# Seven products in place of eight for the second FFN product of chunks 2 to 6

## The chip, the cores and the metric

The kernel runs on one core of a Trainium2 chip. The metric is the time of one execution on the device, in microseconds (us). Each engine (PE for matmuls, DVE, ACT and POOL for work on elements, SP for DMA issues) takes its instructions from a queue of its own, and they wait for each other by semaphores.

## The reference

Eight batches of eight heads with 576 tokens each go through windowed attention; the heads' outputs side by side are the 4608 x 512 input `x` of a gated FFN.

```python
mask_plain = (rel >= 0) & (rel < 32)                        # heads 0 to 3
mask_dil = (rel >= 0) & (rel < 128) & (rel % 4 == 0)        # heads 4 to 7
attn = softmax(where(mask, q @ k.T / 8, -1e9));  x = heads of (attn @ v), joined
out = (gelu(x @ w_gate) * (x @ w_val)) @ w_out              # 512 -> 1536 -> 512
```

## The kernel before, in words

The FFN goes through nine chunks of 512 tokens, 0 to 8. A chunk has two stages on PE.

The **G stage** (L616 to L623) computes twelve blocks `nb` of 128 hidden columns. A block takes four matmuls of 512 columns for the gate and four for the value (`kc` 0 to 3, one for each quarter of `x` transposed, `xT`), each half in a PSUM bank that `gate_banks` (L816) names, which even and odd blocks use in turn. ACT then computes gelu of the gate (`g`, L872), and DVE multiplies it with the value into `u_all` (`u`, L877).

The **out stage** multiplies `u_all` with `w_out`. In chunks 1 to 6 it does so directly: four token tiles of twelve matmuls of 512 columns in banks 0 and 7 in turn, each tile copied out by ACT or DVE (`store`, L638; words w0, w1, w2, e3) and sent by SP. Chunks 7 and 8 (`SEVEN`, L822) cut both matrices into 2 x 2 blocks and compute seven block products of twelve matmuls of 256 columns, instead of eight (L674 to L706). For that DVE forms sums of neighbouring u blocks (`k`, L662) and once, in chunk 6, sums of the weights (`K`, L647); the partial results go through `snap` (three SBUF tiles), `part_out` (words q0 to q6) and `part_sum` (words s0 to s2).

The attention of batch c+1 lies in the out stage of chunk c (c = 1 to 6), as four pairs of heads i, j, k, l. S computes scores (PE), P takes their exp (ACT), M masks (DVE), D the denominators (PE), l and r their log and the exp of its negative (ACT), N the numerators (PE), and X divides into `xT` (DVE). So chunk c+1's G stage can't finish its first blocks before the last X of chunk c; `firsts` (L970) gives the order of its first sixteen matmuls. In batch 3 (chunk 2) pairs k and l are plain heads, from batch 4 on dilated ones.

The order of all work is written out by hand as words (`gate_words` L910, `out_words` L935), which `run_program` emits one by one. A number means so many of the stage's matmuls; any other word puts its instructions at the end of their engines' queues. Nothing reorders them afterwards. A chunk's loads (`F`, `H`, in chunk 2 `R`) stand at the head of its G words: SP issues the loads of q, k (staged in f32), the DMA transposes of their f16 copies, and the loads of v, for the batch after next; its queue then takes the chunk's output stores. POOL casts the staged q, k to f16, and v (`cast_part`, L302). Batch 4's v is cast at the end of `load_rest` (L298 to L300); for batches 5 to 7 the words v0 (dilated half) and v1 (plain half) in the out stages of chunks 3 to 5 do it.

The output rows of chunk 8 end with `last_products` (L742), which computes the seventh product in three parts, so that the last store is small.

Of the kernel before, what the change touches and what calls it, by code (L numbers as in the profile page):

```python
# [10 lines left out]
F32 = mybir.dt.float32  # L11
# [10 lines left out]
def kernel(  # L22
# [679 lines left out]

    def seven(banks):

        order = ((1, 3, True), (0, 4, True), (1, 5, False), (0, 1, False), (1, 2, True), (0, 7, False), (1, 6, True))
        return [mm for b, kind, first in order for mm in products(banks[b], kind, first)]  # L706

    def part_out(c, what, eng, banks):

        src, by = ps[:, banks[0 if what in (1, 3, 5) else 1], :], 1.0 / USCALE  # L710
        m3, a, f = snap
        dst = {0: m3, 1: a, 3: f}.get(what)
        osb = None
        if dst is None:
            osb = osbp.tile([P, DM], F32, tag="osb")
            dst = osb
        if what < 4:
            if eng:
                nc.scalar.activation(dst, src, AF.Copy, bias=0.0, scale=by)  # L719
            else:  # L720
                nc.vector.tensor_scalar(dst, src, by, None, ALU.mult)
        else:
            other, op = {4: (a, ALU.add), 5: (m3, ALU.subtract), 6: (f, ALU.add)}[what]
            nc.vector.scalar_tensor_tensor(dst, src, by, other, ALU.mult, op)  # L724
# [6 lines left out]
    def part_sum(what, eng):  # L731

        m3, a, f = snap
        e = nc.vector if eng else nc.gpsimd
        if what == 0:
            e.tensor_tensor(f, f, m3, ALU.add)  # L736
        elif what == 1:
            e.tensor_tensor(m3, tiles["O", 2], m3, ALU.subtract)
        else:
            e.tensor_tensor(f, f, tiles["O", 4], ALU.subtract)  # L740

    def last_products(c):  # L742

        for p, c0, c1, bank in ((0, 0, HM, 3), (1, 0, P, 5), (1, P, HM, 6)):
            for j, (s, t) in enumerate(operands(6)):
                src = ps[:, bank, 0 : c1 - c0]
                nc.tensor.matmul(src, s[:, P * p : P * p + P], t[:, c0:c1], start=j == 0, stop=j == NKP - 1)
            osb = osbp.tile([P, DM], F32, tag="osb")
            dst, rest = osb[:, 0 : c1 - c0], snap[2][:, HM * p + c0 : HM * p + c1]
            nc.vector.scalar_tensor_tensor(dst, src, 1.0 / USCALE, rest, ALU.mult, ALU.add)  # L750
            t0 = c * CH + 256 + P * p
            (nc.scalar if c0 else nc.sync).dma_start(out=out[t0 : t0 + P, HM + c0 : HM + c1], in_=dst)
# [100 lines left out]
    def run_program(c, words, mms, banks):  # L853

        units = {"S": two_s, "M": two_m, "D": two_den, "N": two_num, "T": two_t, "B": two_b, "X": two_x, "A": two_a, "l": two_l, "r": two_r, "P": two_p_of, "t": turn_first, "y": turn_second, "c": cast_six, "W": idle, "b": bias_first}
        joint = {"S": two_s_mms, "D": two_den_mms, "N": two_num_mms}
        for word in words.split():
            kind, args = word[0], [] if "+" in word else [int(x) for x in word[1:].split("@") if x]
            if "+" in word:
                lists = []  # L860
                for part in word.split("+"):
                    n, at = (int(x) for x in part[1:].split("@"))
                    lists.append((joint[part[0]](n, at), odd(n)))
                emit_tiles(*lists)
            elif kind.isdigit():
                for _ in range(int(word)):
                    mms.pop(0)()
            elif kind in units:
                units[kind](*args)
            elif kind == "g":  # L870
                g = ffn.tile([P, CH], F16, tag="g")
                nc.scalar.activation(g, ps[:, gate_banks(c, args[0])[0], :], AF.Gelu)  # L872
                tiles["g", args[0]] = g
            elif kind == "u":
                nb = args[0]
                val = ps[:, gate_banks(c, nb)[1], :]
                nc.vector.scalar_tensor_tensor(u_all[:, nb, :], tiles.pop(("g", nb)), USCALE, val, ALU.mult, ALU.mult)  # L877
            elif kind in "ew":
                at = args[1] if len(args) > 1 else c
                store(at, args[0], out_banks(at)[args[0]], "act" if kind == "e" else "dve")  # L880
            elif kind == "k":
                u_sums(*args)
            elif kind == "K":
                weight_sums(*args)
            elif kind == "q":
                part_out(c, args[0], args[1], banks)
            elif kind == "s":
                part_sum(*args)
            elif kind == "L":
                mms.clear()  # L890
                last_products(c)
            elif kind == "V":
                (second, second_v)[args[0] if args else 0]()
            elif kind == "v":
                cast_part(c + 2, args[0], tiles["M"])
            elif kind == "F":
                load_first(args[0])
            elif kind == "H":
                load_rest(args[0])
            elif kind == "R":  # L900
                load_rest(3)
                load_first(4)
                load_rest(4)
            elif kind == "E":
                nc.scalar.preload_act_table_set("natural_log_exp_and_others")
            else:
                nc.scalar.preload_act_table_set("gelu_and_others")  # L907
        assert not mms

    def gate_words(c):  # L910
# [22 lines left out]
        return f"{before} {loads} 7 G 3 g0 1 u0 1 g1 4 u1{sums[1]} {rest} 4 g{NNB - 1} 4{last}"  # L933

    def out_words(c):  # L935

# [19 lines left out]
        first = f"1 u11 4 S{i}@1+S{j}@4 E P{i} P{j} M{i} M{j} 7 w0 5" if c < 3 else f"E P{i} P{j} 1 u11 M{i} M{j}{v0} 12 w0 3"
        after = f"S{l + 1}@12+S{l + 2}@15" if 1 < c < 6 else ""
# [50 lines left out]
```

## Time and profile before

| | |
|---|---|
| median of 3 runs | 325.67 us (325.59 to 326.34) |
| profiled execution | 325.92 us, span 324.2 us |
| PE busy | 317.5 us, 98% of the span |
| DVE, ACT, POOL busy | 173.6, 159.1, 87.7 us |
| a G stage | 20.72 us on PE |
| out stages of chunks 2, 3 to 5, 6, 7 | 14.07, 13.30 to 13.31, 12.91, 9.17 us |

The span runs from the first to the last instruction; the time has 1.7 us more around it. Stages are read off the chain of work that ended last, which lists PE's groups with their starts. A matmul's shown end includes its way through the array, so a short one behind long ones ends a little early and the next long one a little late; only sums over a stage are exact.

### The profile page before, as it was taken

How to read it: one execution, taken by the hardware profiler on the slowest of the kernel's cores; microseconds unless marked ns; L12 is line 12 of the kernel's file. 1: busy time of each engine (PE TensorE's matmuls, PEld its weight loads, DVE VectorE, ACT ScalarE, POOL GpSimd, SP SyncE). 2: the span in 40 equal slices, each digit the busy share in tenths (PEclk: the TensorE clock that was granted, in tenths of full speed). 3: DMA queues.
4: the chain of work that ended last, by engine and by line, in shares of the span. 5: the costliest groups of instructions: out<-in, count | busy, mean ns of one | idle time of the engine just before them, and what ended most of it. 6: DMA issues, size and time to landing. Idle time of an engine off the chain costs nothing.

```text
span 324.2 us, 7943 instructions
## 1 busy us (share of the span) xinstructions
PE 317.5 (98%) x3273; PEld 162.6 (50%) x3273; DVE 173.6 (54%) x287; ACT 159.1 (49%) x239; POOL 87.7 (27%) x138
## 2 busy tenths in 40 slices
PE   7999999999999999999999999999999999999995
PEld 4754544444544454445444454445444544684474
DVE  6764646435543355436543554446676467636654
ACT  2673567434653557347633764366535753333320
POOL 8785703402491422231124111411000000040001
PEclk9999999999999999999999999999999999999999
DMA  8999997998899898898389627973000210021003
GB/s 190 183 198 207 205 192 154 268 185 193 194 253 207 214 198 237 191 223 183 126 191 242 161 78 178 249 169 111 32 3 0 92 42 0 0 84 47 2 1 129
DMA packets 107700, 47.11 MB, mean 145 GB/s; under 512 B 83600, under 2 KB 104080, under 8 KB 107664
## 3 DMA queue, kind: packets, MB, share of 16 engines
q1 hardware_dynamic: 94160, 38.29, 51.1%
q0 software_dynamic: 12944, 7.67, 16.6%
q10 hardware_dynamic: 560, 0.66, 0.7%
q8 instruction: 25, 0.41, 0.5%
q14 instruction: 11, 0.09, 0.1%
HBM read 37.75 MB, written 9.44 MB: 146 GB/s over the span
## 4 chain that ended last, share of the span: by engine, by line
PE 92%; DMA 4%; DVE 1%; POOL 1%; issue 0%; DVEq 0%
PE ps L623 58%; PE ps L630 23%; PE ps L458 6%; PE ps L696 5%; DMA wg<-in_moe_w_gate_dram 2%; DMA xT<-in_q_dram 2%; POOL xT L182 0%; DVE turned L740 0%; PE ps L378 0%; DVE osb L724 0%; PE ps L398 0%; DVE osb L750 0%; POOL band L123 0%; DVE ones L67 0%; PE ps L447 0%
## 5 line engine op out<-in xcount | busy, mean ns | idle before, releaser
L877 DVE SCALAR_TENSOR_TENSOR u_all<-g,ps 128x512 f16<-128x512 f16 x108 | 74.2, 688 | 93.3 <-PE ps L623 76.2
L872 ACT ACTIVATE g<-ps 128x512 f16<-128x512 f32 x108 | 63.6, 597 | 105.3 <-PE ps L623 105.3
L623 PE MATMUL ps<-xT,wg 128*128 128x512 f16 x432 | 112.5, 379 | 0.2 <-DMA wg<-in_moe_w_gate_dram 0.2
L623 PE MATMUL ps<-xT,wv 128*128 128x512 f16 x432 | 112.3, 379 | 0.0
L630 PE MATMUL ps<-wo,u_all 128*128 128x512 f16 x336 | 77.8, 380 | 0.0
L623 PEld LDWEIGHTS <-wv 128*128 128x128 f16 x432 | 42.1, 98 | 51.0 <-DMA wv<-in_moe_w_val_dram 0.6
L623 PEld LDWEIGHTS <-wg 128*128 128x128 f16 x432 | 42.1, 98 | 50.5 <-DMA wg<-in_moe_w_gate_dram 0.3
L630 PEld LDWEIGHTS <-u_all 128*128 128x128 f16 x336 | 30.8, 98 | 35.6 <-issue 0.5
L614 DVE TENSOR_TENSOR xT<-ps,rb 128x576 f16<-128x576 f32 x32 | 28.7, 936 | 16.2 <-PE ps L458 12.9
L488 ACT ACTIVATE P<-ps 128x832 f16<-128x832 f32 (+1 forms) x32 | 25.3, 835 | 15.8 <-PE ps L458 15.7
L217 POOL CAST s<-stage 128x640 f16<-128x640 f32 x24 | 17.3, 747 | 53.5 <-DMA stage<-in_q_dram 38.9
L254 POOL CAST v<-stage 128x1152 f16<-128x1152 f32 x11 | 13.0, 1184 | 62.0 <-DMA stage<-in_v_dram 43.5
L585 ACT ACTIVATE lg<-ps 128x576 f32<-128x576 f32 x30 | 18.7, 653 | 11.4 <-DVE xT L614 8.8
L591 ACT ACTIVATE rb<-lg 128x576 f32<-128x576 f32 x30 | 19.5, 690 | 0.3
L736 POOL TENSOR_TENSOR turned<-turned,vdiag 128x512 f32<-128x512 f32 x1 | 1.3, 1262 | 65.6 <-ACT turned L719 65.6
L229 POOL CAST s<-stage 128x512 f16<-128x512 f32 x24 | 14.4, 629 | 8.6 <-DMA stage<-in_q_dram 6.7
L643 DVE TENSOR_SCALAR osb<-ps 128x512 f32<-128x512 f32 x21 | 14.4, 685 | 2.6 <-PE ps L630 2.0
L493 DVE TENSOR_TENSOR P<-P,two_p 128x832 f16<-128x832 f16 x14 | 8.6, 612 | 10.9 <-ACT P L488 10.9
L493 DVE TENSOR_TENSOR P<-P,two_d 128x768 f16<-128x768 f16 x14 | 9.1, 664 | 9.8 <-ACT P L488 9.2
L907 ACT ACT_TABLE_LOAD x9 | 11.5, 1283 | 0.2
L458 PEld LDWEIGHTS <-v 64*64 64x64 f16 x616 | 7.7, 107 | 6.2 <-issue 5.1
L458 PEld LDWEIGHTS <-q 64*64 64x64 f16 x576 | 7.9, 107 | 5.3 <-issue 3.7
(90 smaller groups left out, 208.0 us busy)
## 6 DMA issues: line engine op xcount, KB each, us to landing
out_dram<-osb SPq DMA_DIRECT2D x35, 256.0 KB, 2.2
stage<-in_v_dram SPq DMA_DIRECT2D x28, 144.0 KB, 3.6
stage<-in_q_dram SPq DMA_DIRECT2D x24, 128.0 KB, 3.6
stage<-in_k_dram SPq DMA_DIRECT2D x24, 128.0 KB, 2.9
stage<-in_q_dram SPq DMA_DIRECT2D x6, 512.0 KB, 5.1
stage<-in_k_dram SPq DMA_DIRECT2D x6, 512.0 KB, 5.3
stage<-in_v_dram SPq DMA_DIRECT2D x20, 128.0 KB, 2.9
wo<-in_moe_w_out_dram POOLq DMA_DIRECT2D x3, 512.0 KB, 16.2
```

The lines of the kernel that those rows point to most:

```text
L217: nc.gpsimd.tensor_copy(s16[:, 1280 * t + 640 * g : 1280 * t + 640 * g + 640].rearrange("p (k c) -> p k c", k=5), st_of(i).rearrange("p (k ...
L458: nc.tensor.matmul(o[cols], lhs[rows], rhs[rows], start=st, stop=end, skip_group_check=True)
L488: nc.scalar.activation(pt[:, 0 : src.shape[1]], src, AF.Exp, bias=0.0, scale=scale)
L493: tiles["M"] = nc.vector.tensor_tensor(pt, pt, mask, ALU.mult)
L585: nc.scalar.activation(lg, psf[:, c0 : c0 + S], AF.Ln)
L591: nc.scalar.activation(rb, tiles.pop(("lg", n)), AF.Exp, scale=-1.0)
L614: nc.vector.tensor_tensor(dst, num, rb, ALU.mult)
L623: nc.tensor.matmul(ps[:, bank, :], w[:, kc, ns], xT[kc][:, tok], start=first, stop=end)
L630: nc.tensor.matmul(ps[:, bank, :], u_all[:, fc, tb * P : (tb + 1) * P], wo_t[fc // 4][:, fc % 4, :], start=(fc == 0), stop=(fc == NNB - 1),)
L696: lambda s=s, t=t, p=p, st=first and j == 0 and p == 0, end=j == NKP - 1: nc.tensor.matmul(ps[:, bank, HM * p : HM * p + HM], s[:, P * p : ...
L872: nc.scalar.activation(g, ps[:, gate_banks(c, args[0])[0], :], AF.Gelu)
L877: nc.vector.scalar_tensor_tensor(u_all[:, nb, :], tiles.pop(("g", nb)), USCALE, val, ALU.mult, ALU.mult)
```

## The change

The seven-product scheme is used in chunks 2 to 8. What goes with it:

- The products come in another order, M4, M5, M1, M3, M7, M2, M6, in two banks in turn. M5 is copied out before M3 is added onto its bank, so a partial M5 is kept; likewise M4 before M1. In chunks 2 to 6 q1 and q3 are on ACT and the other copies on DVE; s0 to s2 are on POOL. In chunk 7 s0 to s2 are on DVE.
- `part_sum` always adds into the third tile of `snap`: M4 + M1, minus M5, plus the second quarter of the output, minus the third one. q6 adds M6 to it.
- The sums of the weights move from chunk 6 to chunk 1, and the out stages of chunks 2 to 6 are redrawn: all four S of a batch stand in its own out stage, and none for the next.
- Batch 4's v is no longer cast in `load_rest` but by v0 and v1 in chunk 2's out stage; v0 and v1 now stand behind s1 and ahead of s2 in the words.
- Odd blocks use banks 3 and 6 instead of 1 and 4, and the first sixteen matmuls of chunks 3 to 7 have new orders.
- Chunk 8 has an out stage of its own, `last_chunk`, over banks 1, 2, 4, 5 and at the end 0, 7, 2, with M7 last in three parts.

```diff
-        if b < 5:
+        if b < 4:
             for part in range(0 if by_pool else 2):
                 cast_part(b, part)
...
-        order = ((1, 3, True), (0, 4, True), (1, 5, False), (0, 1, False), (1, 2, True), (0, 7, False), (1, 6, True))
+        order = ((1, 4, True), (0, 5, True), (1, 1, False), (0, 3, False), (1, 7, False), (0, 2, True), (1, 6, True))
...
-        dst = {0: m3, 1: a, 3: f}.get(what)
...
+        kept = {0: 0, 1: 1, 2: 2}.get(what)
...
-            other, op = {4: (a, ALU.add), 5: (m3, ALU.subtract), 6: (f, ALU.add)}[what]
+            other, op = {4: (snap[1], ALU.subtract), 5: (snap[0], ALU.add), 6: (snap[2], ALU.add)}[what]
...
+    def part_sum(what, eng, behind=0):
+
+        other, op = ((snap[1], ALU.subtract), (tiles.get(("O", 3)), ALU.add), (tiles.get(("O", 5)), ALU.subtract))[what]
+        ins = (nc.vector if eng else nc.gpsimd).tensor_tensor(snap[2], snap[2], other, op)
+        if behind:
+            tc.add_manual_dep(ins.ins, tiles["M"].ins.name, SYNC, reason="masks first")
+
+    def last_chunk(c):
...
+        run(2, 4, True)
+        nc.scalar.activation(a, ps[:, 2, :], AF.Copy, bias=0.0, scale=by)
+        run(5, 5, True)
+        nc.scalar.activation(e, ps[:, 5, :], AF.Copy, bias=0.0, scale=by)
+        run(1, 2, True)
+        c21 = osbp.tile([P, DM], F32, tag="osb", name="c21")
+        nc.vector.scalar_tensor_tensor(c21, ps[:, 1, :], by, a, ALU.mult, ALU.add)
+        sends(c21, 5)
+        run(2, 1, False)
+        nc.scalar.activation(f, ps[:, 2, :], AF.Copy, bias=0.0, scale=by)
+        run(5, 3, False)
+        nc.vector.tensor_tensor(f, f, e, ALU.subtract)
+        nc.vector.tensor_tensor(a, f, c21, ALU.subtract)
+        c12 = osbp.tile([P, DM], F32, tag="osb", name="c12")
+        nc.scalar.activation(c12, ps[:, 5, :], AF.Copy, bias=0.0, scale=by)
+        sends(c12, 3)
+        nc.vector.tensor_tensor(a, a, c12, ALU.add)
+        run(4, 6, True)
+        c22 = osbp.tile([P, DM], F32, tag="osb", name="c22")
+        nc.vector.scalar_tensor_tensor(c22, ps[:, 4, :], by, a, ALU.mult, ALU.add)
+        sends(c22, 6)
+        for p, c0, c1, bank in ((0, 0, HM, 0), (1, 0, P, 7), (1, P, HM, 2)):
...
-        return ((0, 7), (1, 6) if c == 1 else (1, 4))[nb % 2]
+        return ((0, 7), (1, 6) if c == 1 else (3, 6))[nb % 2]
-    SEVEN = range(7, NCH)
+    SEVEN = range(2, NCH)
...
+        first = "12 G 1 g0 1 g1 2 u0 u1" if 2 < c < 8 else "7 G 3 g0 1 u0 1 g1 4 u1"
...
-            return f"12 q0@1 12 q1@1 12 q2@0 12 q3@1 s0@{c - 7} s1@0 12 q4@0 s2@{c - 7} 12 q5@0 {tail}"
+            return "12 q0@1 12 q1@1 12 q2@1 s0@1 12 q3@1 s1@1 12 q4@0 12 q5@0 s2@1 12 q6@0" if c < NCH - 1 else "L"
...
-        v0, v1 = (" v0", " v1") if 2 < c < 6 else ("", "")
+        v0, v1 = (" v0", " v1") if 1 < c < 6 else ("", "")
...
+                f"3 S{i}@1+S{j}@4 E P{i} P{j} u11 k5@0 k5@1 k5@2 9 q0@0 M{i} M{j} 10 S{k}@1+S{l}@4 2 P{k} q1@1 P{l} M{k} "
+                f"4 D{i}@11+D{j}@41 8 M{l} q2@0 s0@0@1 12 l{i} l{j} r{i} r{j} N{i}@10+N{j}@40 D{k}@12+D{l}@42 q3@1 s1@0{v0}{v1} "
+                f"l{k} l{l} X{i} X{j} r{k} r{l} 12 q4@0 10 N{k}@13+N{l}@43 2 q5@0 s2@0 X{k} 12 q6@0 X{l}"
...
+    orders[4] = "002 003 102 103 112 113 000 100 110 012 013 010 001 101 111 011"
+    orders[5] = "000 001 100 101 110 111 002 102 112 010 011 012 003 103 113 013"
+    firsts = {c: orders[c if c < 3 else 4 if c == 3 else 5 if c < 8 else 3] for c in range(NCH)}
```

In a word of `firsts`, the digits are block, gate (0) or value (1), and `kc`.

More of the change, by code (lines that the diff above doesn't have):

```diff
@@ L710, in part_out @@
         src, by = ps[:, banks[0 if what in (1, 3, 5) else 1], :], 1.0 / USCALE
-        m3, a, f = snap
-        dst = {0: m3, 1: a, 3: f}.get(what)
-        osb = None
-        if dst is None:
+        kept = {0: 0, 1: 1, 2: 2}.get(what)
+        if kept is None:
             osb = osbp.tile([P, DM], F32, tag="osb")
             dst = osb
+        else:
+            dst = snap[kept]
         if what < 4:
@@ L722, in part_out @@
         else:
-            other, op = {4: (a, ALU.add), 5: (m3, ALU.subtract), 6: (f, ALU.add)}[what]
+            other, op = {4: (snap[1], ALU.subtract), 5: (snap[0], ALU.add), 6: (snap[2], ALU.add)}[what]
             nc.vector.scalar_tensor_tensor(dst, src, by, other, ALU.mult, op)
-        if osb is not None:
+        if kept is None:
             tiles["O", what] = osb
-            t0, d0 = c * CH + 256 * (what in (4, 6)), HM * (what in (2, 6))
+            t0, d0 = c * CH + 256 * (what in (5, 6)), HM * (what in (3, 6))
@@ L728, in part_out @@
             dram = out[t0 : t0 + 256, d0 : d0 + HM].rearrange("(p r) d -> r p d", r=P)
             nc.sync.dma_start(out=dram, in_=osb.rearrange("r (p d) -> r p d", p=2))
[L731 to L740, printed above, removed]
@@ L742, in last_products @@
-    def last_products(c):
-        for p, c0, c1, bank in ((0, 0, HM, 3), (1, 0, P, 5), (1, P, HM, 6)):
-            for j, (s, t) in enumerate(operands(6)):
+    def part_sum(what, eng, behind=0):
[3 more added lines that the diff above has]
+            tc.add_manual_dep(ins.ins, tiles["M"].ins.name, SYNC, reason="masks first")
@@ new lines, in last_chunk, with run, sends @@
+    def last_chunk(c):
+        by = 1.0 / USCALE
+        a, e, f = snap
+        def run(bank, kind, first):
+            for mm in products(bank, kind, first):
+                mm()
+        def sends(tile, what):
+            t0, d0 = c * CH + 256 * (what in (5, 6)), HM * (what in (3, 6))
+            dram = out[t0 : t0 + 256, d0 : d0 + HM].rearrange("(p r) d -> r p d", r=P)
+            nc.sync.dma_start(out=dram, in_=tile.rearrange("r (p d) -> r p d", p=2))
+        run(2, 4, True)
[20 more added lines that the diff above has]
+        for p, c0, c1, bank in ((0, 0, HM, 0), (1, 0, P, 7), (1, P, HM, 2)):
+            for j, (s, t) in enumerate(operands(7)):
@@ L748, in last_products @@
             osb = osbp.tile([P, DM], F32, tag="osb")
[L749 to L752, printed above, removed]
+            dst, rest = osb[:, 0 : c1 - c0], f[:, HM * p + c0 : HM * p + c1]
+            nc.vector.scalar_tensor_tensor(dst, src, by, rest, ALU.mult, ALU.add)
+            t0 = c * CH + P * p
+            (nc.scalar if c0 else nc.sync).dma_start(out=out[t0 : t0 + P, c0:c1], in_=dst)
     def warm(n, bank, rows=P, cols=CH):
@@ L890, in run_program @@
                 mms.clear()
-                last_products(c)
+                last_chunk(c)
             elif kind == "V":
@@ L932, in gate_words @@
         last = f" u{NNB - 1} k5@0 k5@1 k5@2" if c > 6 else ""
-        return f"{before} {loads} 7 G 3 g0 1 u0 1 g1 4 u1{sums[1]} {rest} 4 g{NNB - 1} 4{last}"
+        first = "12 G 1 g0 1 g1 2 u0 u1" if 2 < c < 8 else "7 G 3 g0 1 u0 1 g1 4 u1"
+        return f"{before} {loads} {first}{sums[1]} {rest} 4 g{NNB - 1} 4{last}"
     def out_words(c):
@@ L969 @@
     }
-    firsts = {c: orders[c if c < 3 else 2 if c == 3 else 3] for c in range(NCH)}
+    orders[4] = "002 003 102 103 112 113 000 100 110 012 013 010 001 101 111 011"
+    orders[5] = "000 001 100 101 110 111 002 102 112 010 011 012 003 103 113 013"
+    firsts = {c: orders[c if c < 3 else 4 if c == 3 else 5 if c < 8 else 3] for c in range(NCH)}
     def run_chunk(c):
```

7 lines of the change are left out of this document (removed).

## Prediction

> **What bounds the kernel now.** I read the page first, then the stages, then the chain of waits, then the queues around chunk 2. The page and the stages (us, then busy time and count of PE, PEld, DVE, ACT, POOL, then clock, DMA share, GB/s):
>
> ```profile
> span 324.2 us, 7943 instructions
> PE 317.5 (98%) x3273; PEld 162.6 (50%) x3273; DVE 173.6 (54%) x287; ACT 159.1 (49%) x239; POOL 87.7 (27%) x138
> ...
> 110.67:124.74 14.07, 14.07 (x282) 7.25 (x280) 8.19 (x12) 8.87 (x13) 4.77 (x7) 1.00 0.98 213
> 124.74:145.46 20.72, 20.72 (x97) 9.37 (x96) 7.95 (x12) 9.15 (x15) 6.55 (x10) 1.00 1.01 229
> 145.46:158.76 13.30, 13.30 (x257) 6.83 (x256) 8.30 (x12) 8.97 (x13) 2.71 (x2) 1.00 0.73 159
> 213.50:226.81 13.31, 13.31 (x258) 6.85 (x256) 7.59 (x12) 8.98 (x13) 2.29 (x2) 1.00 0.49 134
> 247.53:260.44 12.91, 12.91 (x221) 6.47 (x220) 7.36 (x12) 8.97 (x13) 0.00 (x0) 1.00 0.18 63
> 260.44:281.16 20.72, 20.72 (x98) 9.43 (x97) 13.47 (x28) 8.94 (x14) 0.00 (x0) 1.00 0.04 13
> 281.16:290.33 9.17, 9.17 (x85) 8.16 (x84) 3.61 (x7) 3.07 (x4) 3.14 (x3) 1.00 0.17 59
> ```
>
> PE has no gap in any stage, at full clock: it is the bound, and whatever it is spared counts until another engine holds it up. Rows two to five below are the out stages of chunks 2, 3, 5 and 6 (chunk 4 is like 5); the last is the seven-product stage of chunk 7: 84 matmuls in 9.17 us, without attention.
>
> **The saving on PE.** The chain of waits has chunk 6's out stage in pieces (start, us, what), with one S burst of chunk 2 ahead:
>
> ```profile
> 111.75 0.47 PE ps L458 x36
> ...
> 247.53 3.45 PE ps L630 x16
> 250.98 0.85 PE ps L458 x64
> 251.83 2.91 PE ps L630 x13
> 254.75 0.87 PE ps L458 x63
> ...
> 258.75 0.50 PE ps L458 x43
> ```
>
> A large matmul takes 3.45 / 16 = 0.2156 us, so 48 take 10.35, and the seven products save 1.18 per chunk. The bursts: S of a pair of pairs 0.47; S and D together 0.85, so D 0.38; N and D 0.87; N alone 0.50. The new stage has S, S, D, N with D, and N: 0.47 + 0.47 + 0.38 + 0.87 + 0.50 = 2.69. Behind a burst 13 large ones take 2.91, where 13 x 0.2156 = 2.80: a return costs 0.11 in this way of counting, and the new stage has five. So 9.17 + 2.69 + 5 x 0.11 = **12.4** (11.9 if returns to small matmuls are free). Chunks 3 to 6 take 13.30 + 13.31 + 13.31 + 12.91 = 52.8 now and 49.6 then: **-3.2** (-5.2 with free returns). Chunk 2 drops from 14.07 to 12.4.
>
> **What the saving meets in chunk 2.** Queues of SP and POOL there (start, us, engine, line), and the landing of the loads of plain v (L241, batches 4 and 5):
>
> ```profile
> 109.31 7.50 SPq L272 DMA_TRANSPOSE q<-s  x4
> 116.90 3.24 SPq L246 DMA_DIRECT2D stage<-in_v_dram  x4
> ...
> 121.48 2.66 SPq L241 DMA_DIRECT2D stage<-in_v_dram  x4
> 124.24 2.58 SPq L645 DMA_DIRECT2D out_dram<-osb  x4
> 126.87 2.80 SPq L210 DMA_DIRECT2D stage<-in_q_dram  x4
> ...
> DMA to landing us min/median/max: 2.8/3.6/4.6
> ...
> 123.11 1.15 POOL L254 CAST v<-stage 128x1152 f16<-128x1152 f32 x1 [7.43 <-DMA stage<-in_v_dram]
> 127.94 1.15 POOL L254 CAST v<-stage 128x1152 f16<-128x1152 f32 x1 [3.68 <-DMA stage<-in_v_dram]
> ...
> 287.12 1.26 POOL L736 TENSOR_TENSOR turned<-turned,vdiag 128x512 f32<-128x512 f32 x1 [65.56 <-ACT turned L719]
> 289.76 0.69 DVE L724 SCALAR_TENSOR_TENSOR osb<-ps,vdiag 128x512 f32<-128x512 f32 x1 [1.26 <-POOL vdiag L738]
> ```
>
> The plain half of batch 4's v is the last of chunk 2's loads, and its cast waited for the DMA until 127.94. Today nobody waits for that cast before chunk 4. In the new words POOL has s0, s1, v0, v1, s2 in this order: s2 stands behind v1, q6 (DVE) needs s2, and behind q6 on DVE stand the X of pair l and all u of chunk 3. q6 frees bank 7. Chunk 3's new order (002 003 102 103 112 113 000 100 110 **012**) writes bank 7 with its tenth matmul.
>
> SP's queue up to these loads is the same in both kernels, and the DMA share in this stretch is 0.98 and 1.01, so I let v land when it does now. Then v1 ends at 127.94 + 1.15 = 129.1, s2 at 130.35, q6 at 131.05, with the handoffs (0.09 each, below) 131.2. PE ends chunk 2 at 110.67 + 12.4 = 123.1, does nine matmuls (1.94) until 125.0, and stands for 6.2 us. Now the tenth matmul starts at 124.74 + 1.94 = 126.7. Net **+4.5**, in which chunk 2's own saving is already used up. Landing after 2.8 in place of 4.4 us (the last of four issues starts near 123.5) makes it +2.9; POOL casts that DVE's new sums hold up make it up to +5.5.
>
> **The clock.** A hole that long has another price. PE's first work, its first large matmuls, an early warm one, and the end of the kernel:
>
> ```profile
> 1.53 3.84 PE L757 MATMUL ps<-ones 128*32 128x32 f16 x73 [1.53 <-DVE ones L67]
> 7.20 0.38 PE L763 MATMUL ps<-ones 128*128 128x512 f16 x1
> ...
> L757 PE MATMUL ps<-ones 128*128 128x512 f16 x4 | 1.9, 627 | 0.0
> ...
> 318.74 1.49 PE L747 MATMUL ps<-wx,u_all 128*128 128x256 f16 x18
> ...
> 323.10:323.20 0.10, 0.00 (x0) 0.00 (x0) 0.00 (x0) 0.00 (x0) 0.00 (x0) 0.83 0.00 0
> 323.20:323.30 0.10, 0.00 (x0) 0.00 (x0) 0.00 (x0) 0.00 (x0) 0.00 (x0) 0.50 0.00 0
> ```
>
> PE's last matmul ends at 320.23 and the granted clock falls to 0.50 near 323.17, after 2.9 idle us. At the start, four cold matmuls of 512 columns stand (1.9 - 0.627) / 3 = 0.42 us apart, twice 0.2156, and the clock came up between 3.84 and 5.67 us after the first work (5.37 the end of the cold group, 7.20 a matmul of 0.38). Half speed for so long loses 1.9 to 2.8; none if the clock stays up. I take **+2.2**. [...]
>
> **The other boundaries.** Rows of ACT and DVE in chunks 5, 7 and 8:
>
> ```profile
> 214.58 1.62 ACT L488 ACTIVATE P<-ps 128x832 f16<-128x832 f32 x2
> 217.72 1.51 ACT L488 ACTIVATE P<-ps 128x768 f16<-128x768 f32 x2 [1.52 <-PE ps L458]
> 219.12 1.20 ACT L585 ACTIVATE lg<-ps 128x576 f32<-128x576 f32 x2
> 220.18 1.28 ACT L591 ACTIVATE rb<-lg 128x576 f32<-128x576 f32 x2
> 225.53 2.16 DVE L614 TENSOR_TENSOR xT<-ps,rb 128x576 f16<-128x576 f32 x2 [1.58 <-PE ps L458]
> ...
> 282.53 0.41 DVE L672 TENSOR_TENSOR u_all<-u_all 128x512 f16<-128x512 f16 x1
> ...
> 282.56 0.60 ACT L719 ACTIVATE vdiag<-ps 128x512 f32<-128x512 f32 x1 [1.64 <-PE ps L696]
> ```
>
> Time t from the end of the G stage. PE: 3 matmuls, S, 9 and 10 until 3.0, S until 3.45, 2 until 3.8 (M1), 4, D and 8 until 5.6 (M3), 12 until 6.9, N with D until 7.8, M7 until 9.2, M2 with N until 11.1, M6 until 12.4. DVE has u11 and the k5 sums done at 1.8 (282.94 - 281.16), then q0 (0.69) at 2.6, before M1 needs its bank at 3.8. ACT: P of i, j until 2.7; P of k at 3.5; from there P, l, r lasted 3.74 (217.72 to 221.46), with q1's 0.60 until 7.8 (q1 itself by 5.0, M3 needs it at 5.6); q3 until 8.4, M2 needs that bank at 9.2. POOL: s1 until 9.7, v0 and v1 until 12.0, s2 until 13.3 (q5 is done by 11.9, so the casts keep s2 waiting 0.1); q6 until 14.0, X of l (1.08) until 15.1. PE needs q6 at 12.4 + 1.94 = 14.3 and that X at the thirteenth matmul, 12.4 + 2.59 = 15.0: 0.1 late, and the g that then frees bank 0 another 0.1. Four boundaries: **+0.8** (0 to 3: chains this close give way by 0.7 each if ACT is that late).
>
> Chunk 7: q5 starts at 7.96, then s2 and q6 follow, three times 0.69 to 10.05; chunk 8's fourth matmul needs bank 3 at 9.17 + 0.65 = 9.82: **+0.3** (0 to 0.4).
>
> The k sums of chunks 2 to 6 and the weights' sums cost nothing while DVE has room: chunk 7's G stage carries the k sums at 13.47 of 20.72 us with PE gapless. Were POOL's casts to hold them up by a cast each, u would still come before its bank is used again, three half blocks (2.59) later; without that slack each costs its own 0.4. The stores carry the same bytes.
>
> **The end.** Today DVE is late with the last sums:
>
> ```profile
> 318.36 1.24 DVE L740 TENSOR_TENSOR turned<-turned,osb 128x512 f32<-128x512 f32 x1
> ...
> 320.12 0.82 DVE L750 SCALAR_TENSOR_TENSOR osb<-ps,turned 128x256 f32<-128x256 f32 x3
> ```
>
> It ends at 320.94, 0.7 behind PE's 320.23. `last_chunk` has its sums done before M7 ends; the last third of these 0.82 then follows PE's end by the handoff of 0.09 (M3 of chunk 7 ends at 281.16 + 1.31 = 282.47, ACT starts at 282.56): 320.6, **-0.3** (-0.4 to 0).
>
> **The sum:** 4.5 + 2.2 - 3.2 + 0.8 + 0.3 - 0.3 = +4.3 on the profiled 325.92 (span 324.2 and 1.7 around it), 330.2; that execution is 0.25 above the median of 325.67, so **330.0**.
>
> **The rivals.** *B, the clock holds:* the hole is there, but no 2.2: 327.8. For it: one fall in the whole trace, at the end. *C, no hole (the other side):* v lands in time for s2. Then chunk 2 saves 14.07 - 12.4 = 1.7 too: -1.7 - 3.2 + 1.0 (five boundaries) + 0.3 - 0.3 = -3.9, **321.8**. It decides from v1 starting before 125.0 - 3.2 = 121.8, which is 6 us earlier than now; against it speak the full DMA queue and that SP only issues these loads from 121.48 on. It would also be so if POOL did s2 ahead of v1; no row shows an overtaking. [...] *D, queues too full:* ACT is busy 8.97 + 2 x 0.60 = 10.2 of 12.4 us, and q3 sits behind two P, two l and two r; against it, q3's slack of 0.8. If that is gone and all behind it slips, 0.7 more at four boundaries: 332.8.
>
> **How the numbers follow.** Forecast 0.55, B 0.17, C 0.16, D 0.12. Range 326.0 to 332.6: from B with an early landing (327.8 - 1.6) to D; left out are C and little else. The likeliest case alone: 328.2 to 331.5. About 0.3% (1 us) is what can be told from no change. Slower by that 0.78 (forecast, D, most of B), within it 0.05 (B's low end), faster 0.17 (C).
>
> **What would show it.** Right: one gap of some 6 us on PE early in chunk 3's G stage, released by DVE's q6, behind POOL's s2 and a v cast that waited for DMA to about 128; a granted clock below 1 there; out stages of 12.4. Wrong: PE gapless from 123 to 131, or v cast before 122.

## The result and the profile after

The changed kernel takes **338.32 us** (336.83 to 340.02, four runs) against 325.84 for the kernel before beside it: ratio 1.0383 [1.0332, 1.0434] (95% interval in brackets). The forecast was 330.0 in 326.0 to 332.6: slower, as said, but by three times as much. The profiled execution took 338.51, 12.59 more than the profiled one of before.

The head of the page, and then the stages of the changed kernel (us, busy time and count of PE, PEld, DVE, ACT, POOL, then clock, DMA share, GB/s):

```profile
span 336.8 us, 8410 instructions
PE 320.1 (95%) x3453; PEld 182.2 (54%) x3453; DVE 214.7 (64%) x389; ACT 162.5 (48%) x246; POOL 103.0 (31%) x149
```

```profile
110.59:125.20 14.61, 13.07 (x282) 10.63 (x280) 10.75 (x15) 11.32 (x16) 8.41 (x10) 1.00 0.98 202
...
127.13:131.44 4.31, 0.00 (x0) 0.00 (x0) 0.74 (x2) 0.00 (x0) 2.37 (x2) 0.89 0.57 193
131.44:134.90 3.46, 3.46 (x9) 1.22 (x9) 0.82 (x2) 1.08 (x2) 0.00 (x0) 0.50 0.67 174
134.90:153.25 18.35, 18.35 (x82) 8.06 (x81) 12.44 (x26) 6.19 (x11) 5.48 (x9) 0.94 0.87 205
153.25:167.20 13.95, 12.85 (x293) 10.48 (x292) 8.45 (x15) 11.24 (x16) 5.17 (x5) 1.00 0.33 85
167.20:188.32 21.12, 21.02 (x98) 9.44 (x97) 16.08 (x29) 7.26 (x13) 6.88 (x10) 1.00 0.95 204
188.32:202.25 13.93, 12.83 (x294) 10.51 (x292) 8.42 (x15) 11.25 (x16) 5.14 (x5) 1.00 0.45 110
...
258.48:272.40 13.92, 12.82 (x293) 10.49 (x292) 8.42 (x15) 11.24 (x16) 2.96 (x3) 1.00 0.12 41
272.40:293.55 21.15, 21.06 (x99) 9.43 (x97) 14.32 (x29) 7.06 (x12) 0.86 (x1) 1.00 0.08 26
...
302.72:323.93 21.21, 20.88 (x99) 9.41 (x97) 13.21 (x28) 7.06 (x12) 0.00 (x0) 1.00 0.08 25
323.93:336.80 12.87, 9.19 (x91) 8.13 (x88) 5.93 (x12) 2.39 (x4) 0.00 (x0) 0.94 0.25 83
```

Two things are to be seen. PE stands for 4.31 us in chunk 3's G stage and runs at half clock after it. And the out stages of chunks 3 to 6, which were to shrink to 12.4 us, are longer than before, with PE idle for 1.1 us in each. Against before, stage by stage:

| part | forecast | measured |
|---|---|---|
| chunk 2's out stage and the hole | +4.5 | 0.54 + 4.31 = +4.85 |
| clock | +2.2 | 153.25 - 125.20 - 20.72 - 4.31 = +3.02 |
| out stages of chunks 3 to 6 | -3.2 | 55.73 - 52.83 = +2.90 |
| G stages of chunks 4 to 7 | +0.8 (with all at these boundaries) | 84.57 - 82.88 = +1.69 |
| chunk 8's G stage | +0.3 | 21.21 - 20.72 = +0.49 |
| tail | -0.3 | 12.87 - 13.15 = -0.28 |

The clock's 3.02 is a remainder of chunk 3's G stage and holds its small waits too. These make 12.67; chunk 2's out stage began 0.08 earlier. Of the 8.3 us between forecast and result, 6.1 lie in the four out stages.

**The hole.** The timelines of PE, POOL and DVE around it:

```profile
126.75 0.38 PE L623 MATMUL ps<-xT,wv 128*128 128x512 f16 x1
131.44 1.44 PE L623 MATMUL ps<-xT,wv 128*128 128x512 f16 x3 [4.31 <-DVE osb L724]
...
123.83 1.14 POOL L254 CAST v<-stage 128x1152 f16<-128x1152 f32 x1 [2.55 <-DMA stage<-in_v_dram]
128.29 1.15 POOL L254 CAST v<-stage 128x1152 f16<-128x1152 f32 x1 [3.31 <-DMA stage<-in_v_dram]
129.40 1.26 POOL L734 TENSOR_TENSOR turned<-turned,osb 128x512 f32<-128x512 f32 x1
...
130.70 0.69 DVE L724 SCALAR_TENSOR_TENSOR osb<-ps,turned 128x512 f32<-128x512 f32 x1 [5.43 <-POOL turned L734]
```

This is the chain of the prediction: v1 (L254) waits for its DMA until 128.29, s2 (L734) follows it on POOL, q6 (L724) follows s2, and the tenth matmul starts at 131.44. The clock, us by us:

```profile
129.00:130.00 1.00, 0.00 (x0) 0.00 (x0) 0.00 (x0) 0.00 (x0) 1.00 (x2) 1.00 0.44 154
130.00:131.00 1.00, 0.00 (x0) 0.00 (x0) 0.30 (x1) 0.00 (x0) 0.66 (x1) 0.73 0.00 0
131.00:132.00 1.00, 0.56 (x2) 0.25 (x2) 1.00 (x2) 0.00 (x0) 0.00 (x0) 0.50 0.00 0
...
136.00:137.00 1.00, 1.00 (x4) 0.35 (x3) 0.96 (x3) 0.60 (x1) 0.00 (x0) 0.50 0.55 125
137.00:138.00 1.00, 1.00 (x6) 0.41 (x5) 0.18 (x1) 0.00 (x0) 0.52 (x1) 0.86 1.00 227
```

0.73 is 0.46 us at full and 0.54 at half speed, so the clock fell at 130.46, 3.3 us after the shown end of the last matmul. (A large one alone is shown with 0.38 us, where in a row they start 0.2156 apart.) By the same reading of 0.86 it came back at 137.28, 5.8 us after PE resumed; half of that is 2.9. The two changes are 6.83 us apart. In run 2 below, where PE resumes at 132.24, its matmuls start 0.43 us apart from 133.48 to 136.89 and 0.215 apart from 138.43 on. At the end of the changed kernel's execution the last matmul ends at 333.12, and the clock falls at 335.26, 2.1 us after it.

**The out stages.** PE, ACT and DVE in chunk 3's:

```profile
156.18 0.54 PE L458 MATMUL ps<-q 64*64 64x96 f16 x36
156.65 0.39 PE L696 MATMUL ps<-wo,ux 128*128 128x256 f16 x2
156.88 0.60 PE L696 MATMUL ps<-wx,ux 128*128 128x256 f16 x4
157.62 0.23 PE L458 MATMUL ps<-P,ones 64*64 64x96 f16 x2
158.81 0.57 PE L458 MATMUL ps<-P,ones 64*64 64x96 f16 x26 [0.96 <-ACT P L488]
...
156.76 0.81 ACT L488 ACTIVATE P<-ps 128x768 f16<-128x768 f32 x1 [0.80 <-PE ps L458]
157.46 0.59 ACT L719 ACTIVATE vdiag<-ps 128x512 f32<-128x512 f32 x1
157.94 0.82 ACT L488 ACTIVATE P<-ps 128x768 f16<-128x768 f32 x1
...
155.81 1.08 DVE L493 TENSOR_TENSOR P<-P,two_p 128x832 f16<-128x832 f16 x2
163.34 1.42 DVE L614 TENSOR_TENSOR xT<-ps,rb 128x576 f16<-128x576 f32 x2 [2.25 <-ACT lg L585]
...
162.65 1.19 ACT L585 ACTIVATE lg<-ps 128x576 f32<-128x576 f32 x2 [0.30 <-PE ps L458]
```

S of k and l ends at 156.7, P of k follows at once, then q1 (L719), then P of l. D of i starts when P of k ends (157.57), D of j when P of l ends (158.76). Yet what D reads, P of *i* and *j* behind their masks (L493), was ready at 156.89. What D and the later P share is a PSUM bank: by `win` and `base_of`, S of l stands in columns 2112 to 2879 and D of j in 2880 to 3455, both partly in bank 5; S of k and D of i meet in bank 2 in the same way. No column overlaps. It isn't ACT's queue as a whole that D waits for: D of i starts while q1 is running and before P of l, which both stand ahead of it in the words. The same holds for X of i (L614), whose idle time of 2.25 us ends with l of k (L585, the first of the two): N of i and D of k share bank 2, and X and l both only read. Again X of i doesn't wait for l of l, which runs until 163.84. Some 0.7 of the 2.25 us are l of k's, which starts at 162.65; before that, PE is still at D of k and l.

In the words of before, D stands ahead of P, and X ahead of l. There the wait is on the other side, as one row of ACT in that trace shows:

```profile
154.49 0.65 ACT L585 ACTIVATE lg<-ps 128x576 f32<-128x576 f32 x1 [0.98 <-DVE xT L614]
```

That the bank is what they share is read from the columns; no run moved a tile to another bank with the order kept. So the theory: 7 us come from v1 ahead of s2, and the rest from the order of the words, which sets who waits for whom in a shared bank. The rival: the attention's engines are simply too full for a 12.4 us stage (case D), and moving words doesn't help.

### The profile page after: what moved, and what is told of

Read it like the earlier page. It is cut to its first block, busy times and chain, and to the rows that moved or that the text cites. A ratio compares the mean times of both kernels' runs of the same rounds, so it can differ in the third digit from the quotient of the medians.

```text
span 336.8 us, 8410 instructions
## 1 busy us (share of the span) xinstructions
PE 320.1 (95%) x3453; PEld 182.2 (54%) x3453; DVE 214.7 (64%) x389; ACT 162.5 (48%) x246; POOL 103.0 (31%) x149
## 4 chain that ended last, share of the span: by engine, by line
PE 80%; DMA 5%; DVE 4%; ACT 3%; SPq 2%; POOL 2%; issue 2%; POOLq 0%; DVEq 0%
PE ps L623 53%; PE ps L696 13%; PE ps L630 6%; PE ps L458 6%; DVE osb L724 2%; DMA q<-s 2%; ACT P L488 2%; DMA xT<-in_k_dram 2%; DVE xT L614 2%; POOL turned L734 2%; DMA stage<-in_v_dram 1%; SPq L246 1%; PE ps L378 1%; ACT vdiag L719 1%; DMA out_dram<-c 1%
## 5 line engine op out<-in xcount | busy, mean ns | idle before, releaser
L623 PE MATMUL ps<-xT,wv 128*128 128x512 f16 x432 | 114.2, 383 | 4.3 <-DVE osb L724 4.3
L623 PE MATMUL ps<-xT,wg 128*128 128x512 f16 x432 | 114.0, 382 | 0.8 <-DVE osb L724 0.3
L614 DVE TENSOR_TENSOR xT<-ps,rb 128x576 f16<-128x576 f32 x32 | 29.1, 936 | 14.6 <-ACT lg L585 11.2
L696 PE MATMUL ps<-wx,u_all 128*128 128x256 f16 x240 | 30.4, 273 | 0.0
L734 POOL TENSOR_TENSOR turned<-turned,vdiag 128x512 f32<-128x512 f32 x5 | 6.4, 1274 | 69.0 <-ACT rb L591 69.0
L696 PEld LDWEIGHTS <-ux 128*128 128x128 f16 x252 | 23.4, 98 | 3.5
L585 ACT ACTIVATE lg<-ps 128x576 f32<-128x576 f32 x30 | 18.2, 649 | 9.7 <-PE ps L458 5.6
L630 PE MATMUL ps<-wo,u_all 128*128 128x512 f16 x96 | 22.4, 380 | 0.0
L696 PE MATMUL ps<-wo,ux 128*128 128x256 f16 x168 | 22.2, 273 | 0.0
L666 DVE TENSOR_TENSOR ux<-u_all 128x512 f16<-128x512 f16 x42 | 20.4, 486 | 1.4
L254 POOL CAST v<-stage 128x1152 f16<-128x1152 f32 x11 | 12.6, 1161 | 24.6 <-DMA stage<-in_v_dram 24.6
L229 POOL CAST s<-stage 128x512 f16<-128x512 f32 x24 | 16.0, 695 | 7.8 <-DMA stage<-in_q_dram 5.2
L672 DVE TENSOR_TENSOR u_all<-u_all 128x512 f16<-128x512 f16 x42 | 17.9, 426 | 0.0
L493 DVE TENSOR_TENSOR P<-P,two_d 128x768 f16<-128x768 f16 x14 | 9.2, 667 | 8.3 <-ACT P L488 8.3
```

What stands on the lines that cost most here:

```text
L585: nc.scalar.activation(lg, psf[:, c0 : c0 + S], AF.Ln)
L614: nc.vector.tensor_tensor(dst, num, rb, ALU.mult)
L623: nc.tensor.matmul(ps[:, bank, :], w[:, kc, ns], xT[kc][:, tok], start=first, stop=end)
L630: nc.tensor.matmul(ps[:, bank, :], u_all[:, fc, tb * P : (tb + 1) * P], wo_t[fc // 4][:, fc % 4, :], start=(fc == 0), stop=(fc == NNB - 1),)
L666: nc.vector.tensor_tensor(ux[:, j, 1:3].rearrange("p s t -> p (s t)"), k0, k1, ALU.add)
L672: nc.vector.tensor_tensor(flat, two[:, :, 256:512], two[:, :, 0:256], ALU.subtract)
```

## The experiments

Diffs are against the changed kernel unless another is named.

**1. v0 and v1 behind s2.**

```diff
-                f"4 D{i}@11+D{j}@41 8 M{l} q2@0 s0@0@1 12 l{i} l{j} r{i} r{j} N{i}@10+N{j}@40 D{k}@12+D{l}@42 q3@1 s1@0{v0}{v1} "
-                f"l{k} l{l} X{i} X{j} r{k} r{l} 12 q4@0 10 N{k}@13+N{l}@43 2 q5@0 s2@0 X{k} 12 q6@0 X{l}"
+                f"4 D{i}@11+D{j}@41 8 M{l} q2@0 s0@0@1 12 l{i} l{j} r{i} r{j} N{i}@10+N{j}@40 D{k}@12+D{l}@42 q3@1 s1@0 "
+                f"l{k} l{l} X{i} X{j} r{k} r{l} 12 q4@0 10 N{k}@13+N{l}@43 2 q5@0 s2@0{v0}{v1} X{k} 12 q6@0 X{l}"
```

> One edit to the changed kernel: in the out stages of chunks 2 to 5 the casts v0 and v1 stand behind s2 on POOL, not ahead of it. Theory (s2, and with it q6, X of pair l and the tenth matmul of chunk 3, waits for v1's cast, which waits for the DMA until about 128): PE's gap of 4.3 us at 127.1 goes, and with it the 3.0 us at half clock behind it; at 0.4 for an ordinary boundary the time is 338.3 - 6.9 = 331.4, ratio to the kernel before about 1.017, granted clock 1.00 in chunk 3. Rival 1 (q6 is late for another reason, such as DVE's queue): 338. Rival 2 (the casts, now later, hold up the loads of the batch after, and the gap moves to a later chunk): 334 to 338 with a gap in chunks 4 to 6.

Measured: **331.20**, ratio 1.0172 [1.0157, 1.0188], as expected. POOL's timeline and the stage of the former hole:

```profile
124.76 1.26 POOL L734 TENSOR_TENSOR turned<-turned,osb 128x512 f32<-128x512 f32 x1 [3.48 <-DVE osb L724]
126.75 1.14 POOL L254 CAST v<-stage 128x1152 f16<-128x1152 f32 x1 [0.73 <-DMA stage<-in_v_dram]
```

```profile
125.20:145.90 20.70, 20.66 (x96) 9.30 (x95) 16.65 (x29) 7.05 (x12) 9.06 (x12) 1.00 0.98 227
```

s2 runs as soon as q5 is done, the hole is gone, the clock stays at 1.00: 7.1 us for two words. The other 5.5 us stay. The chain of waits has the long run of matmuls in the G stages of chunks 4 and 5, from whose starts the time of a whole chunk is read, here and in the other runs:

```profile
163.81 17.43 PE ps L623 x80
...
198.88 17.43 PE ps L623 x80
```

A chunk takes 35.07 us, as in the changed kernel; before it was 158.76 - 124.74 = 34.02.

**2. D of i and j ahead of P of k and l, as in the words of before.**

```diff
-                f"3 S{i}@1+S{j}@4 E P{i} P{j} u11 k5@0 k5@1 k5@2 9 q0@0 M{i} M{j} 10 S{k}@1+S{l}@4 2 P{k} q1@1 P{l} M{k} "
-                f"4 D{i}@11+D{j}@41 8 M{l} q2@0 ...
+                f"3 S{i}@1+S{j}@4 E P{i} P{j} u11 k5@0 k5@1 k5@2 9 q0@0 M{i} M{j} 10 S{k}@1+S{l}@4 D{i}@11+D{j}@41 2 P{k} q1@1 P{l} M{k} "
+                f"12 M{l} q2@0 ...
```

> One edit to the changed kernel: in the out stages of chunks 2 to 6 the denominators D of pairs i and j stand right behind the scores S of k and l, ahead of P of k and l, as they did in the kernel before; all 12 matmuls of M1 follow. Theory (D of j stands on PE behind ACT's P of l, because both use one PSUM bank, 1.0 us per out stage in the trace): the wait goes, and each out stage of chunks 3 to 6 drops from 13.9 to 12.7 or so; chunk 2's share is eaten by the gap in chunk 3. 338.3 - 4 x 1.2 = 333.5, ratio 1.023. Rival (ACT's queue is the bound of the out stage, and the wait only moves to the next burst, to M2 behind q3 or to the start of the G stage): 337 to 338, with new waits of PE for ACT or DVE of about 1 us per chunk.

Measured: **336.45**, ratio 1.0335 [1.032, 1.0351], 3 us above the expectation and nearer to the rival's 337. PE's waits for ACT's P are gone from the list; in their place stand (us in total, times, longest):

```profile
PE ps L623 <- DVE osb L724: 5.2, 2, 4.9
...
PE ps L458 <- DVE xT L614: 1.4, 5, 0.8
PE ps L458 <- DVE P L493: 1.4, 5, 0.7
```

Now D comes early enough to wait for the mask of P of j (0.2 in chunks 3 to 6), and N of l waits for X of j. A chunk takes 34.24 us, 0.83 less. In chunk 2 nothing is won, since the tenth matmul of chunk 3 hangs on v1 and starts even later (132.24).

**3. Both.** The edits of 1 and 2 together.

> Both edits: v0 and v1 behind s2, D ahead of P. If the two causes are separate and each is as told, 338.3 - 6.9 - 5 x 1.2 = 325.4, ratio 0.999, no PE gap over 1 us, out stages of 12.7. If ACT's queue is the bound of the out stage, 331 (only the first edit counts). If the boundaries then lose more because the out stage is shorter, 327 to 329.

Measured: **327.95**, ratio 1.0078 [1.0061, 1.0095]: 10.4 us better than the change, where 1 and 2 alone give 7.1 and 1.9; the 1.4 above their sum (1.1 in the profiled executions) are what run 2 could not show: its tenth matmul came 0.8 later, and chunk 2's out stage takes 14.51 us here and 14.81 in run 1. It is 2.6 us above the expectation. The same rows of the chain:

```profile
162.68 17.43 PE ps L623 x80
...
196.92 17.43 PE ps L623 x80
```

34.24 a chunk again, so the new small waits of run 2, which the expectation left out, are here too.

**4. The hole filled with work.** 22 matmuls of ones go into the unused bank 2 ahead of the tenth matmul of chunk 3; nobody uses what they write.

```diff
-        first = "12 G 1 g0 1 g1 2 u0 u1" if 2 < c < 8 else "7 G 3 g0 1 u0 1 g1 4 u1"
+        fill = "9 " + "W1@2@0 " * 22 + "3" if c == 3 else "12"
+        first = f"{fill} G 1 g0 1 g1 2 u0 u1" if 2 < c < 8 else "7 G 3 g0 1 u0 1 g1 4 u1"
```

> The changed kernel with 22 idle matmuls of 512 columns (4.7 us, into bank 2, which nothing else uses then) ahead of the tenth matmul of chunk 3's G stage, where PE stands 4.3 us. Their results are not used. Theory (the gap costs its 4.3 us and then 3.0 more, because the clock falls to 0.50 and needs 6 us of work to come back): the tenth matmul starts at about 131.9 in place of 131.4, the clock stays at 1.00 and the time is 338.3 - 3.0 + 0.4 = 335.7, ratio 1.030. Rival (what is lost after the gap is lost to other engines starting late, not to the clock): 338.5 or more.

Measured: **336.74**, ratio 1.0344 [1.0325, 1.0364]. The stretches from the ninth matmul on:

```profile
127.13:132.14 5.01, 4.83 (x24) 2.06 (x22) 0.75 (x2) 0.00 (x0) 2.37 (x2) 1.00 0.58 185
132.14:135.60 3.46, 3.42 (x16) 1.46 (x16) 2.24 (x5) 1.68 (x3) 0.00 (x0) 1.00 0.68 175
```

The clock stays at 1.00 with PE busy for 4.83 of the 5.01 us, and behind the hole the same 3.46 us hold 16 matmuls, not 9. The tenth matmul came 0.7 us later here (q6 did), so of the 3.0 us, 1.6 show in the median and 0.7 went into that. The two medians' runs spread over 3.2 and 1.6 us, so this agrees with 3.0 and doesn't measure it. In the profiled executions the stretch from the tenth matmul to the end of the stage takes 21.81 us in the changed kernel and 19.15 here (132.14 to 151.29): 2.7 us less where the clock stays up.

**5. Masks of i and j ahead of q0** (against run 3), for the wait of D on the mask.

```diff
-... k5@2 9 q0@0 M{i} M{j} 10 S{k}@1+S{l}@4 ...
+... k5@2 9 M{i} M{j} q0@0 10 S{k}@1+S{l}@4 ...
```

> e3_both with one more edit: in the out stages of chunks 2 to 6, M of i and j stand ahead of q0 on DVE. In e3 the D of i and j wait 0.2 us for M of j, which stands behind q0 (0.69), and N of l waits 0.16 for X of j. Theory (the out stage is now bound by the chain P, M, D, P of k, q1, P of l, l, r, X): the chain starts 0.3 earlier, both waits go, a period of chunks 3 to 6 drops from 34.24 to 33.8 or so, 327.95 - 5 x 0.4 = 326.0, ratio 1.001. Rival (q0, now later, keeps M1 from its bank): no gain, 328.

Measured: **326.66**, ratio 1.0026 [1.0011, 1.0041]; 33.94 a chunk, 0.3 less than in run 3 (33.8 was expected). Its seven runs lie from 325.69 to 327.36, which no row explains.

**6. X of l ahead of q6** (against run 3), so that the last quarter of `xT` doesn't wait for s2. The first blocks then take that quarter early and bank 7 last.

```diff
-... s2@0{v0}{v1} X{k} 12 q6@0 X{l}"
+... s2@0{v0}{v1} X{k} X{l} 12 q6@0"
-    orders[4] = "002 003 102 103 112 113 000 100 110 012 013 010 001 101 111 011"
-    orders[5] = "000 001 100 101 110 111 002 102 112 010 011 012 003 103 113 013"
+    orders[4] = "002 003 102 103 112 113 000 100 110 001 101 111 012 013 010 011"
+    orders[5] = "000 001 100 101 110 111 002 102 112 003 103 113 010 011 012 013"
...
-        first = "12 G 1 g0 1 g1 2 u0 u1" if 2 < c < 8 else ...
+        first = "9 G 1 g0 1 g1 5 u0 u1" if 2 < c < 8 else ...
```

> e3_both with one more edit, at the boundaries into chunks 3 to 7: X of l stands ahead of q6 on DVE, and the first sixteen matmuls of the G stage come in an order that needs this X first (tenth) and q6's bank last (thirteenth), with g0 after the tenth. Theory (the chain q5, s2 on POOL, q6, X of l is 0.2 late, and g0 behind the thirteenth matmul 0.2 more): 0.4 per boundary goes, a period drops from 34.24 to 33.84, 327.95 - 5 x 0.4 = 326.0, ratio 1.001. Rival (q6 is now the late one by as much): 327.5 to 328.5.

Measured: **327.19**, ratio 1.0045 [1.0032, 1.0059], 1.2 us above the expectation and just under the rival's 327.5; 33.97 a chunk. The chunks do gain 0.27 each, but chunk 2's out stage took 14.94 us in the profiled execution (14.51 in run 3), which no run took apart.

**7. Runs 5 and 6 together, and chunk 8's first two blocks one after the other.**

```diff
+        if c == NCH - 1:
+            first = "4 G g0 4 u0 4 g1 4 u1"
...
+    orders[6] = "000 001 002 003 010 011 012 013 100 101 102 103 110 111 112 113"
...
-    firsts = {c: orders[c if c < 3 else 4 if c == 3 else 5 if c < 8 else 3] for c in range(NCH)}
+    firsts = {c: orders[c if c < 3 else 4 if c == 3 else 5 if c < 8 else 6] for c in range(NCH)}
```

> Both edits of e5 and e6, and chunk 8's first blocks in plain order (bank 3 from the ninth matmul on, not the fourth). Theory: PE has no wait over 0.1 us left from chunk 3 on, a period of chunks 3 to 6 is 20.72 + 12.5 = 33.2 to 33.4, chunk 8 gains 0.4 more: 327.95 - 2.0 - 2.0 - 0.4 = 323.5, ratio 0.993 to the kernel before: then the seven products do pay, and the loss was the order of the other engines' work. Rival (the other engines are too full for a shorter out stage, whatever the order): 326 or more.

Measured: **324.78**, ratio 0.9972 [0.9962, 0.9981]: ahead of the kernel before, by about as much as can be told. Chunk 3's out stage and X of i in it:

```profile
145.40:158.20 12.80, 12.64 (x293) 10.51 (x292) 8.44 (x15) 11.01 (x16) 3.00 (x3) 1.00 0.74 177
```

```profile
154.52 1.42 DVE L614 TENSOR_TENSOR xT<-ps,rb 128x576 f16<-128x576 f32 x2 [2.08 <-ACT lg L585]
156.00 0.57 PE L458 MATMUL ps<-P,v 64*64 64x96 f16 x42 [0.16 <-DVE xT L614]
```

33.66 a chunk and 1.3 us above the expectation. The stage takes 12.80, not 12.4: X is still behind l, and N of l behind X.

**8. q1 behind both P** (against the changed kernel): does D follow P, or something else on ACT?

```diff
-... S{k}@1+S{l}@4 2 P{k} q1@1 P{l} M{k} "
+... S{k}@1+S{l}@4 2 P{k} P{l} q1@1 M{k} "
```

> One edit to the changed kernel: q1 stands behind P of l on ACT, not between P of k and P of l. Theory (D of j waits for P of l): P of l ends 0.5 us earlier, the wait of 1.0 us in each out stage shrinks to 0.5, a period of chunks 3 to 6 drops from 35.07 to 34.5, 338.3 - 3 x 0.5 = 336.8 (chunk 2's share goes into the gap, and part of another), ratio 1.033. Rival (D waits for ACT's queue as such, or M3 then waits for q1): 338.3.

Measured: **336.07**, ratio 1.0314 [1.0299, 1.033]; 34.58 a chunk, where 34.5 was expected. PE's wait there:

```profile
PE ps L458 <- ACT P L488: 2.6, 6, 0.5
```

Without the 0.6 us of q1 ahead of P of l, the longest wait falls to 0.5 (in the changed kernel this group has 5.0 us in 6 times, 1.0 the longest). D follows the end of P, and q1, now behind P and still ahead of D in the words, doesn't hold it up: in chunk 3 D of j starts at 158.88, and q1 runs from 158.72 to 159.32.

**9. X of i and j ahead of l of k and l** (against run 7), the other pair that shares a bank.

```diff
-                f"l{k} l{l} X{i} X{j} r{k} r{l} 12 q4@0 ...
+                f"X{i} l{k} X{j} l{l} r{k} r{l} 12 q4@0 ...
```

> e7_all_orders with one more edit, in the out stages of chunks 2 to 6: X of i and l of k, then X of j and l of l, in place of l, l, X, X. In e7 X of i starts 1.5 us after the r that it needs, at the moment at which l of k ends, and N of l waits 0.4 us for X of j; numerators of i and denominators of k share a PSUM bank. Theory (two engines' accesses to one bank go in the order in which they are written down, even where the columns differ and both only read): X of i then starts 1 us earlier, the 0.4 us wait goes, the out stages are the bare 12.4 that the prediction had worked out, a period drops from 33.66 to 33.3: 324.8 - 5 x 0.4 = 322.8, ratio 0.991. Rival (X waits for ACT's r or its queue as a whole): 324.8, X of i starts no earlier.

Measured: **322.52** (322.11 to 323.21, six runs), ratio 0.9896 [0.9874, 0.9918]; 33.28 a chunk, as expected. Chunk 3's out stage, chunk 4's G stage, and X of i with the work on PE ahead of it:

```profile
145.02:157.43 12.41, 12.41 (x293) 10.39 (x292) 8.43 (x15) 11.07 (x16) 2.93 (x3) 1.00 0.61 164
157.43:178.29 20.86, 20.86 (x99) 9.43 (x97) 16.57 (x29) 7.31 (x14) 9.24 (x12) 1.00 0.89 195
```

```profile
151.84 0.58 PE L458 MATMUL ps<-P,v 64*64 64x96 f16 x40
152.26 0.53 PE L458 MATMUL ps<-P,ones 64*64 64x96 f16 x24
...
152.87 1.42 DVE L614 TENSOR_TENSOR xT<-ps,rb 128x576 f16<-128x576 f32 x2 [0.80 <-PE ps L458]
```

X now waits for PE alone and not for l. Its own N is done by 152.42, but it starts right behind D of k and l (152.79), which stands ahead of it in the words and has columns in the same bank. PE has no gap, and the stage takes 12.41. Between the changed kernel and this one no matmul and no pass over data is taken away: 15.8 us lie in the order of the words, 7.1 in v1 and s2, about 7.2 in chunks 3 to 6 (4 x (35.07 - 33.28)), 0.5 in chunk 8 and the rest in chunk 2. This version takes 1.0% less than the kernel before (0.8 to 1.3% by the interval) and 4.7% less than the changed one. The rival falls: ACT is busy for 11.07 of these 12.41 us and PE doesn't wait for it.

## Why the prediction was right in its direction and wrong in its size

*The saving on PE* was right. Its 12.4 for the new stage is what run 9 measures (12.41, busy without a gap); the 0.11 per return belongs in it. That it agrees to 0.01 is luck in the last digit.

*What the saving meets in chunk 2* was right in mechanism, place and releaser, and run 1 shows it by taking the cause away. The tenth matmul was to start at 131.2 and did at 131.44. The gap itself was shorter, 4.31 and not 6.2, because chunk 2's out stage took 14.61 and not 12.4: time lost ahead of a landing that doesn't hang on it costs nothing more (v1's cast began at 127.94 before and at 128.29 here). Case C is out in both its forms: v did not land in time for s2, and POOL did not run s2 ahead of the waiting v1. POOL did them in the order of the words: v1 at 128.29 and s2 at 129.40 in the changed kernel, s2 at 124.76 and v1 at 126.75 in run 1. DVE held up neither cast of chunk 2: they took 1.14 and 1.15 us, and 1.15 each before; in the kernel before one cast beside DVE's masks took 1.56 (150.62).

*The clock* was right in kind and a little low: 3.0 in place of 2.2, because half speed lasted 5.8 us after PE resumed, where the prediction had 3.84 to 5.67 from the start of the kernel before. That reading rests on the matmuls' distance alone (0.42 us, twice 0.2156): the clock that the trace shows there is 1.00 from 0 to 8 us. Run 4 shows that the fall hangs on PE standing idle: with 4.83 of 5.01 us busy the clock stays at 1.00. How long PE must stand is no single figure here: the clock fell 3.3 us after the last matmul's shown end in the hole, 2.1 us after it at the end of that execution and 2.9 us after it at the end of the kernel before. No run shows what sets this, or the 5.8 us.

*The other boundaries* is the step that failed. Its walk through the queues has on PE "4, D and 8 until 5.6 (M3)", with D at 0.38 and no wait, and has no wait for l at X. It held a reader to the data it reads, not to the PSUM bank it shares. At the start ACT was where the walk had it (S over at t = 3.45, P of k at 3.5), and q3 was in time, so case D, priced by q3, was not the cause either. What the walk lacked: D waits for P of k and then, behind q1, for P of l (0.96 us), and X of i for l of k (0.7 in the changed kernel, 1.3 in run 7, counted from the end of D of k and l). In place of +0.8 for four boundaries, the four out stages came to 13.9 instead of 12.4 (+6.1 in all) and their G stages to +1.69. Runs 3, 5, 7 and 9 undo this piece by piece, from 35.07 to 34.24, 33.94, 33.66 and 33.28 us a chunk; run 2 takes out the wait for P alone and run 8 half of it. The walk alone would have given 12.4 + 20.72 + 0.2 = 33.3. The sign that could have been read was in the kernel before, in the row of l waiting for X above: two readers of different columns, one waiting for the other.

The waits of D for P (0.96 us) and of X for l (2.25 us of DVE's idle time end with it in the changed kernel, 2.08 in run 7) agree with an order by bank, and so do runs 8 and 9: PE's longest wait for P falls to 0.5 us when P of l ends earlier, and X ahead of l waits for PE alone (0.80). Which part of the system set them can't be seen in the trace.

*7 to 8* (+0.3, 0 to 0.4; measured +0.49) came out a little high, and *the end* (-0.3, measured -0.28) was right. Two slips change nothing: case D's 332.8 lay outside the stated 332.6, and batch 4's v is first read by N in chunk 3's out stage, not in chunk 4.

Open: why the changed kernel's four runs spread over 3.2 us when those of before stay within 1.0 (325.36 to 326.34) but for one at 327.75. The clock is part of it: the fastest of the four has a mean granted clock of 0.995 and the others 0.988 to 0.990, which by an estimate from clock and span ((1 - 0.995) x 2 x 335.1) is some 3.4 us at half clock against 7 to 8; but the slowest (340.02) has the same 0.990 as that of 338.13. Open too: why chunk 2's out stage still takes 13.76 in run 9. Its pairs k and l are plain heads, whose P are longer (0.86 and 0.87 us there in the changed kernel, 0.81 and 0.82 in chunk 3), and PE waits 0.7 us there for a mask; no run took that apart.

## What to carry to other kernels

When an order of work is redrawn, walk PSUM by banks: for each bank, list the accesses of all engines in program order, reads among them, and count each as a wait on the one ahead of it, as D behind P (0.96 us) and X behind l (0.7 and 1.3) were here. Put no instruction that waits for a DMA ahead of one that PE needs soon on the same queue (7.1 us in run 1). The gaps here, of 4.3, 4.9 and 5.8 us on PE in the changed kernel and runs 2 and 8, cost 2.4 to 2.7 us more behind them: the 87 matmuls that follow took 21.81, 21.89 and 21.58 us, against 19.15 in run 4 at a clock of 1.00. When PE is the bound, price the bare stage apart from its waits: here the bare price held (12.4, and 12.41 in run 9), and the waits decided whether the seven products paid.

## What the runs showed of the hardware that wasn't expected

Accesses of two engines to one PSUM bank went one after the other in the order of the program, with no column in common and even where both only read: D behind P (0.96 us of PE's time in an out stage), X behind l (0.7 us of DVE's in the changed kernel, 1.3 in run 7), and l behind X in the kernel before (0.98 us of ACT's). That the bank is the unit is read from the columns; no run tested it apart. After a gap of 4.31 us the array ran at half clock for 5.8 us, longer than the gap itself; fall and return were 6.83 us apart.
